# Word conversion at 20 steps an item, six buffers for the first group's columns, GpSimd's DRAIN one row store earlier

## The chip, the cores and the metric

One Trainium2 chip, one NeuronCore. The metric is the device time of one execution in microseconds (us). The engines are named as the profile names them: PE is TensorE (PEld its weight loads), DVE is VectorE, ACT is ScalarE, POOL is GpSimd, SP is SyncE, which here only issues DMAs. SPq and POOLq are the sequencers of SP and POOL.

## The reference, cut to what matters

Pooled attention, then a layer of eight experts of which each token uses one, then a dense layer with the larger of three products. The change lies in the last two.

```python
attn_out = _attn_ref(q, k, v)                       # 8 x 8 heads, 576 tokens, keys pooled by 8
x = attn_out.transpose(0, 2, 1, 3).reshape(4608, 512)
for e in range(8):                                  # experts: 512 -> 1024 -> 512
    mask = expert_idx == e
    h = np.maximum(x[mask] @ w1[e], 0.0)
    out[mask] = gate_w[mask, None] * (h @ w2[e])
h = np.maximum(np.maximum(x @ m1, x @ m2), x @ m3)  # second layer: 512 -> 768, three matrices
return h @ m_out                                    # 768 -> 512
```

## The kernel before

The kernel runs three stages. Attention and routing come first. They are followed by the expert stage: 22 items, of which 18 are pairs (256 tokens) and 4 are singles (128 tokens). Each item has eight pieces, 0 to 3 for the first product (`mm1`, L1090, for singles L1098) and 4 to 7 for the second (`mm2`, L1138, for singles L1122). Every fp32 operand is split into a high and a low part, and three products are taken of the parts. For each piece of a weight, ACT makes `whi` (L1068) and DVE `wlo` (L1070). Behind each `mm1` piece ACT makes `hhi` and DVE `hlo` (L1106). SP loads the raw weights of the next item as soon as a piece has been split.

The second layer's weights are prepared inside the expert stage, in the gaps of DVE and ACT. Two generators do that. `conversions()` (called `cv`) turns the weight words into floats: 48 rows of 256 columns, each row in five steps (L1219, L1232, L1235 with an ACT operation, L1237, L1240). POOL loads the raw words into two buffers, `cvraw`; the load of row n + 2 goes out when L1237 of row n has run (L1238, `load`, L1203). `combinations()` (called `cb`) forms sums and differences of the converted blocks (L1265 to L1278), and POOL stores each 1,792 KB result to `wdram` (L1279). Then it does the same for the output matrix (`wso`, L1302 to L1308), and lastly it runs `columns(0, False)`: the expert stage's result `ybuf` for the first 768 tokens is loaded by SP into `yr` buffers (L1341), six pieces in all, and `sums` (L1358 to L1374) makes the operands `yhl` of the second layer from them.

`between(half, p_)` is called twice in each piece, before and behind its products. When the routing's queue is empty, it advances `cv` by one or two steps and `cb` by one (L1425 to L1427). Whatever is left of both runs behind the last item.

The last stage is `second`: six groups of 768 tokens, nine chunks each. `quad` takes seven products of a chunk into PSUM banks; `snap` (L1688, ACT) copies a partial sum out before a further product is added to its bank; `block` (L1700, L1707, L1708, DVE) forms the maximum of the three matrices. The split of the finished blocks (`ghi` L1727 on ACT, `glo` L1728 and `asum` L1729 on DVE) is kept in the list `parts_` and taken off by `pop(n)` at four points of a quad, by the table `pops` (L1765). `project` multiplies by the output matrix, scales by the gate (`ob`, L1827 on ACT, L1829 on DVE) and stores 128 rows at a time with an indirect DMA of POOL (L1800), six stores in a group. The stores of blocks 0 to 2 follow the products m = 3, those of blocks 3 to 5 the products m = 4. One DRAIN instruction of POOL stands among them (L1833). Each engine takes its instructions in the order of the program.

Of the kernel before, what the change touches and what calls it, by code (L numbers as in the profile page):

```python
# [8 lines left out]
F32 = mybir.dt.float32  # L9
# [12 lines left out]
def attention_moe_moe_kernel(  # L22
# [27 lines left out]
    P = 128  # L50
    B, H, S, D = q.shape
    N, DM = out.shape
    E, _, F = w1.shape
# [66 lines left out]
    if True:  # L120
# [5 lines left out]
        tl = {"w1": [wp1.tile([P, DC, 256], F32, name=f"w1raw{i}") for i in range(4)]}  # L126
# [55 lines left out]
        if True:  # L182
# [761 lines left out]
            def fill(n=1):  # L944

                for _ in range(n):
                    free = [c_ for c_ in queue[0] if c_.state is None] if queue else []
                    if not free:
                        return
                    c_ = free[0]  # L950
                    queue[0].remove(c_)
                    queue[0].append(c_)
                    c_.step()
                    if c_.state == "end":
                        queue[0].remove(c_)
                        if not queue[0]:
                            queue.pop(0)

            def boundary(products=True):

                for c_ in list(queue[0]) if queue else []:
                    if c_.state == "wait":
                        c_.state = None
                    elif c_.state == "pe":
                        c_.state = "products"
                    elif c_.state == "products" and products:
                        c_.step()
# [357 lines left out]
            def columns(g, whole_=True):  # L1325

                w_ = HW if whole_ else HW // 3
                at_ = [(c, n) for c in range(2) for n in range(0, HW, w_)]
                rows = []

                def load(k_):
                    if k_ < len(at_):
                        c, n = at_[k_]
                        t = tl["yr"].tile([P, 2, 2, w_], F32, tag="yr", name=f"yr{g}_{c}_{n}", bufs=2)
                        src = ybuf[:, GW * g : GW * g + GW].rearrange("(i c p) (j n) -> c p i j n", i=2, c=2, j=2)
                        for i in range(2):  # L1340
                            nc.sync.dma_start(t[:, i], src[c, :, i, :, n : n + w_])  # L1341
                        rows.append((t, c, n, w_))

                load(0)
                load(1)
                for _ in range(1 if whole_ else 8):
                    yield
                for k_ in range(len(at_)):
                    yield from sums(*rows[k_])
                    load(k_ + 2)  # L1350

            def sums(t, c, n, w_):
                hi, lo = (x_[:, :, n : n + w_] for x_ in yhl[2 * c : 2 * c + 2])
                tt = nc.vector.tensor_tensor
                b4 = t.rearrange("p i j n -> p (i j) n")
                t_ = tl["yr"].tile([P, 4, w_], F32, tag="ysum", name=uname("ysum"), bufs=1)
                raw = lambda n, m: t_[:, n - 3 : m - 3, :]
                tt(raw(3, 5), b4[:, 1:4:2, :], b4[:, 0:2, :], op=A.subtract)  # L1358
                nc.scalar.copy(hi[:, 0, :], b4[:, 0, :])
                nc.scalar.copy(hi[:, 1:3, :], b4[:, 2:4, :])  # L1360
                yield
                tt(raw(5, 6), b4[:, 3:4, :], raw(3, 4), op=A.subtract)
                tt(raw(6, 7), b4[:, 2:3, :], raw(5, 6), op=A.subtract)
                yield
                nc.scalar.copy(hi[:, 3:7, :], raw(3, 7))
                tt(lo[:, 0, :], b4[:, 0, :], hi[:, 0, :].bitcast(F32), op=A.subtract)
                yield
                tt(lo[:, 1:3, :], b4[:, 2:4, :], hi[:, 1:3, :].bitcast(F32), op=A.subtract)
                yield
                if w_ == HW:  # L1370
                    tt(lo[:, 3:5, :], raw(3, 5), hi[:, 3:5, :].bitcast(F32), op=A.subtract)
                    yield
                n0 = 5 if w_ == HW else 3
                tt(lo[:, n0:7, :], raw(n0, 7), hi[:, n0:7, :].bitcast(F32), op=A.subtract)  # L1374
                yield
# [40 lines left out]
            def between(half, p_=0):  # L1416

                if not routed:
                    return
                if queue:  # L1420
                    if half == 0:
                        boundary(p_ in (0, 1, 2, 3, 7))
                    fill(3)
                else:
                    for _ in range(1 + (p_ % 2 if half else p_ % 4 == 0)):  # L1425
                        next(cv, None)
                    next(cb, None)  # L1427

# [89 lines left out]
            for b in range(1, B):  # L1518
                need = (b // 2) * 9 + (0 if b % 2 == 0 else 4)
                at_ = [need - 7, need - 3, need - 1, need, need, need + 1, need + 2]  # L1520
                at_ = {1: [2, 4, 6, 7], 2: [5, 6, 6, 7, 7, 7, 8, 9, 10]}.get(b, at_[:4] + at_[5:6])
# [102 lines left out]
    CH = F2C // 2 * 3  # L1624
    NCH = CH + 3
    T3 = GB // 2

    def second(st, groups, again=False):
# [10 lines left out]
        def bank(m, name):  # L1639
            x_ = {1: 1, 2: 2, 5: 3}[m]  # L1640
            return pa.tile([P, 512], F32, tag=f"p{x_}", name=name, bufs=2 if x_ == 2 else 3)
# [112 lines left out]
        def quad(g, n, k_):  # L1754
            w_ = wt.pop((g, n))
            nm = f"{g}_{n}"
            p1, p2, p3 = (bank(x_, f"p{x_}_{nm}")[:, 0:HW] for x_ in (1, 2, 5))
            product(p1, w_, 1, True)
            s1 = snap(p1, "s1", f"s1_{nm}")
            product(p3, w_, 5, True)  # L1760
            s5 = snap(p3, "s5", f"s5_{nm}")
            finish_block()
            product(p1, w_, 6, False)
            s2 = snap(p1, "s2", f"s2_{nm}")
            pops = ((3, 1, 1, 3), (1, 0, 0, 0), (0, 0, 1, n < CH - 1))[n % 3]  # L1765
            pop(pops[0])
            product(p2, w_, 2, True)
            block(g, n, (1, 1), (p2, s1))
            pop(pops[1])
            product(p3, w_, 3, False)  # L1770
            block(g, n, (1, 2), (p3, s2))
            pop(pops[2])
            product(p1, w_, 7, False)
            block(g, n, (2, 2), (p1, s5))
            pop(pops[3])

            def last_block():
                product(p1, w_, 4, False)
                load_chunk(k_ + 3)
                block(g, n, (2, 1), (p1,))  # L1780

            late_.append(last_block)
# [29 lines left out]
        def project(g, k0, ahead):  # L1812
            acc, ob = {}, {}
            lo_, hi_ = slice(0, DH), slice(DH, DM)

            def take(m, t):
                if m in (1, 2, 5):
                    acc[m, t] = bank(m, f"o{m}_{g}_{t}")[:, 0:DH]
                if m in (1, 5):
                    j = t if m == 1 else T3 + t  # L1820
                    ob[j] = yp.tile([P, DM], F32, tag="ob", name=f"ob{g}_{j}", bufs=6)
                ps = acc[{1: 1, 6: 1, 7: 1, 4: 1, 5: 5, 3: 5, 2: 2}[m], t]
                out_product(g, m, t, ps)
                j, cols = {1: (t, lo_), 2: (t, lo_), 6: (t, hi_), 3: (t, hi_), 4: (T3 + t, lo_)}.get(m, (T3 + t, hi_))
                dst, gate = ob[j][:, cols], gt[g][:, j : j + 1]
                if m in (1, 5, 6, 4):
                    nc.scalar.activation(dst, ps, AF.Copy, scale=gate)  # L1827
                else:
                    nc.vector.scalar_tensor_tensor(dst, ps, gate, dst, A.mult, A.add)  # L1829
                if m in (3, 4):  # L1830
                    store_rows(g, ob[j], j)
                    if m == 4 and t == 0:
                        nc.gpsimd.drain()  # L1833

            steps = [(1, 0), (1, 1), (5, 0), (1, 2), (5, 1), (5, 2), (6, 0), (6, 1), (6, 2)]
            steps += [(2, 0), (3, 0), (2, 1), (3, 1), (2, 2), (3, 2), (7, 0), (7, 1), (7, 2), (4, 0), (4, 1), (4, 2)]
            for n, (m, t) in enumerate(steps):
                take(m, t)
                if n == 0:
                    pop(3)  # L1840
                elif n == 1:
                    finish_block()
                elif n > 2:
                    pop(3)
                if t == T3 - 1 and m in (6, 3, 4):
                    k_ = (6, 3, 4).index(m)
                    wt.pop((g, CH + k_))
                    load_chunk(k0 + CH + k_ + 3)
                if 5 <= n < 17:
                    next(ahead, None)  # L1850
# [81 lines left out]
```

## Time and profile before

| | |
|---|---|
| median of 3 runs | 1230.9 us (1227.91 to 1232.1) |
| the profiled execution | 1228.26 us, of which the span is 1226.3 us |
| PE busy | 1183.0 us, 96% |
| DVE busy | 884.2 us, 72% |
| ACT busy | 605.4 us, 49% |
| POOL busy | 309.8 us, 25% |

The span is what the profile's clock covers, from the first to the last instruction. The busy time of an engine is the time in which it executes. PE's busy time is drawn from modelled ends of matmuls, so a matmul that is held up shortly can show as a long one.

### The profile page before, as it was taken

The page shows a single profiled execution, that of the slowest core. Times are in us where ns is not written, and L with a number is a line of the kernel's source. Part 1 is how long each engine was busy: PE and PEld are TensorE (multiplying, and loading weights), DVE is VectorE, ACT ScalarE, POOL GpSimd, SP SyncE. Part 2 cuts the span into 40 slices and gives each one's busy share as a digit, 9 for nine tenths or more (in the row PEclk, how much of TensorE's full clock was granted, in tenths as well). Part 3 has the DMA queues.
Part 4 walks back from the last instruction along what each step waited for, and adds up shares of the span by engine and source line. Part 5 has one row for each costly group of instructions (what it writes and reads, how often), then busy time and mean ns, then how long its engine had stood idle before and what let it go on. Part 6 is the DMA issues. An engine that isn't in the chain of part 4 may idle for free.

```text
span 1226.3 us, 23792 instructions
## 1 busy us (share of the span) xinstructions
PE 1183.0 (96%) x8737; PEld 1161.1 (95%) x8737; DVE 884.2 (72%) x1796; ACT 605.4 (49%) x1117; POOL 309.8 (25%) x451
## 2 busy tenths in 40 slices
PE   6899999999999999999999999999999999999997
PEld 5799899999989999999999999999999999999996
DVE  6878977987889999996755368467567557567563
ACT  4666665455666666666655234334334334334332
POOL 7967744201212213213001302104003003003001
PEclk9999999999999999999999999999999999999999
DMA  9998664328865446737539668778769769769763
GB/s 292 241 262 234 176 213 158 121 23 239 277 232 201 148 168 222 265 138 262 177 107 324 233 252 311 290 258 304 283 240 331 260 245 328 272 252 331 267 247 114
DMA packets 108119, 285.10 MB, mean 232 GB/s; under 512 B 17878, under 2 KB 70564, under 8 KB 97628
## 3 DMA queue, kind: packets, MB, share of 16 engines
q1 hardware_dynamic: 87436, 216.40, 51.1%
q0 software_dynamic: 20560, 67.11, 17.8%
q8 instruction: 71, 1.16, 0.4%
q14 instruction: 52, 0.43, 0.1%
HBM read 285.52 MB, written 52.48 MB: 276 GB/s over the span
## 4 chain that ended last, share of the span: by engine, by line
PE 65%; DVE 15%; issue 10%; DMA 5%; ACT 4%; POOL 1%; POOLq 0%; SPq 0%; ACTq 0%; DVEq 0%
PE p L1680 22%; PE py L1138 12%; PE ph L1090 10%; PE o L1792 7%; DVE wlo L1070 3%; PE pav L524 3%; PE ph L1098 2%; PE psc L470 2%; DMA cvraw<-in_moe_w_dram 2%; DVE glo L1728 2%; PE py L1122 2%; PE paT L501 1%; DVE m L1700 1%; PE px L1051 1%; PE pqT L445 1%
## 5 line engine op out<-in xcount | busy, mean ns | idle before, releaser
L1680 PE MATMUL p<-yhi,wt 128*128 128x384 f32 x1512 | 390.4, 337 | 0.6
L1680 PEld LDWEIGHTS p<-yhi,wt 128*128 128x128 f32 x1512 | 273.5, 188 | 4.5 <-ACT s L1688 4.4
L1680 PE MATMUL p<-ylo,wt 128*128 128x384 f32 x756 | 254.1, 336 | 0.0
L1688 ACT COPY s<-p 128x384 f32<-128x384 f32 x162 | 76.5, 480 | 195.9 <-PE p L1680 191.1
L1090 PE MATMUL ph<-xhi,whi 128*128 128x256 f32 x576 | 164.4, 285 | 6.8 <-DVE hlo L1106 5.6
L1090 PE MATMUL ph<-xhi,wlo 128*128 128x256 f32 x576 | 163.2, 283 | 2.1 <-DVE wlo L1070 2.1
L1138 PE MATMUL py<-hhi,wlo 128*128 128x256 f32 x576 | 163.1, 283 | 1.6 <-DVE wlo L1070 1.6
L1138 PE MATMUL py<-hhi,whi 128*128 128x256 f32 x576 | 164.5, 286 | 0.0
L1090 PE MATMUL ph<-xlo,whi 128*128 128x256 f32 x576 | 162.9, 283 | 0.0
L1138 PE MATMUL py<-hlo,whi 128*128 128x256 f32 x576 | 162.9, 283 | 0.0
L1680 PEld LDWEIGHTS p<-ylo,wt 128*128 128x128 f32 x756 | 142.1, 188 | 0.0
L1792 PE MATMUL o<-wt,ghi 128*128 128x256 f32 x756 | 137.6, 283 | 2.2 <-DMA wt<-wdram 0.7
L1707 DVE TENSOR_TENSOR blk<-p,s 128x384 f32<-128x384 f32 x108 | 59.7, 553 | 85.0 <-PE p L1680 85.0
L1792 PEld LDWEIGHTS o<-wt,ghi 128*128 128x128 f32 x756 | 117.2, 189 | 3.9 <-ACT ob L1827 1.6
L1090 PEld LDWEIGHTS ph<-xhi,whi 128*128 128x128 f32 x576 | 110.4, 192 | 8.6 <-DVE hlo L1106 7.3
L1665 POOL DMA_INDIRECT gt<-gbuf,ix x26 | 31.2, 1199 | 325.5 <-DMA ix<-idbuf 187.5
L1090 PEld LDWEIGHTS ph<-xhi,wlo 128*128 128x128 f32 x576 | 110.4, 192 | 2.7 <-DVE wlo L1070 2.7
L1138 PEld LDWEIGHTS py<-hhi,wlo 128*128 128x128 f32 x576 | 110.4, 192 | 2.0 <-DVE wlo L1070 2.0
L1138 PEld LDWEIGHTS py<-hlo,whi 128*128 128x128 f32 x576 | 110.4, 192 | 0.0
L1090 PEld LDWEIGHTS ph<-xlo,whi 128*128 128x128 f32 x576 | 110.4, 192 | 0.0
L1138 PEld LDWEIGHTS py<-hhi,whi 128*128 128x128 f32 x576 | 110.4, 192 | 0.0
L1070 DVE TENSOR_TENSOR wlo<-w2raw,whi 128x1024 fp32r<-128x1024 f32 x84 | 102.2, 1220 | 10.8 <-ACT whi L1068 10.8
(340 smaller groups left out, 2369.2 us busy)
## 6 DMA issues: line engine op xcount, KB each, us to landing
wt<-wdram SPq DMA_DIRECT2D x69, 1792.0 KB
w1raw<-in_moe_w_dram SPq DMA_DIRECT2D x88, 512.0 KB
w2raw<-in_moe_w_dram SPq DMA_DIRECT2D x88, 512.0 KB
wdram<-wst POOLq DMA_DIRECT2D x9, 1792.0 KB
ybuf<-yo SPq DMA_DIRECT2D x40, 256.0 KB
cvraw<-in_moe_w_dram POOLq DMA_DIRECT2D x36, 256.0 KB
xbuf<-x SPq DMA_DIRECT2D x16, 512.0 KB
yr<-ybuf SPq DMA_DIRECT2D x20, 384.0 KB
```

What stands on the lines that cost most here:

```text
L470: nc.tensor.matmul(ps[:, c // 2, (c % 2) * 2 * SP : (c % 2 + 1) * 2 * SP], qT[:, c, :], kbds[segs[0][2] % 3][:, h0 + c].rearrange("p t s - ...
L524: nc.tensor.matmul(ps[lo:hi, bank, (g0 % 4) * DA : (g0 % 4 + g1 - g0) * DA], aT[:, c, lo:hi], vbds[b % 3][:, sl : sl + g1 - g0, :].rearran ...
L1070: eng.tensor_tensor(lo, src, hi.bitcast(F32), op=A.subtract)
L1090: nc.tensor.matmul(ps[:, f, :], a_[:, c, fs], b_[:, c, :], start=(n == 0), stop=(n == 3 * DC - 1))
L1098: nc.tensor.matmul(ps[:, f, 0:P], tl["w1"][piece][:, c, fs], xlo[:, c, 0:P], start=(c == 0), stop=(c == DC - 1))
L1122: nc.tensor.matmul(py[:, 0, :], a_[:, f, 0:P], b_[:, f, :], start=(piece == 0 and f == 0 and n == 0), stop=(last_ and f == 1 and n == 2),)
L1138: nc.tensor.matmul(py[:, c // 2, (c % 2) * 256 : (c % 2 + 1) * 256], a_[:, f, c * P : (c + 1) * P], b_[:, f, :], start=(piece == 0 and f = ...
L1665: nc.gpsimd.indirect_dma_start(out=gt[g][:, j : j + 1], out_offset=None, in_=gbuf[:, :], in_offset=bass.IndirectOffsetOnAxis(ap=cols[j], a ...
L1680: nc.tensor.matmul(ps, a_, b_, start=(start and c + n == 0), stop=(c == 1 and n == 2), skip_group_check=True)
L1688: nc.scalar.copy(t, ps)
L1707: tt(src, add[0], add[1], op=A.add)
L1792: nc.tensor.matmul(ps, a_, b_, start=(m in (1, 2, 5) and c + n == 0), stop=(c == KH - 1 and n == 2), skip_group_check=True,)
```

## The change

Four edits. `between` advances `cv` by one step before each piece's products and by one or two behind them, 20 steps an item; before it was 22, with one more step ahead of pieces 0 and 4. `columns` for the first group allocates six `yr` buffers and issues all six loads at once; before there were two, and each further load went out when a piece had been summed. In `quad` one of the `pop`s of every third chunk moves from behind the third block to ahead of it (this is not in the title). The DRAIN moves from behind the fourth row store (m = 4, t = 0) to behind the third (m = 3, t = 2).

```diff
@@ columns(g, whole_=True)
+                depth = 2 if whole_ else len(at_)
...
-                        t = tl["yr"].tile([P, 2, 2, w_], F32, tag="yr", name=f"yr{g}_{c}_{n}", bufs=2)
+                        t = tl["yr"].tile([P, 2, 2, w_], F32, tag="yr", name=f"yr{g}_{c}_{n}", bufs=depth)
...
-                load(0)
-                load(1)
+                for k_ in range(depth):
+                    load(k_)
                 for _ in range(1 if whole_ else 8):
                     yield
                 for k_ in range(len(at_)):
                     yield from sums(*rows[k_])
-                    load(k_ + 2)
+                    load(k_ + depth)
@@ between(half, p_=0)
-                    for _ in range(1 + (p_ % 2 if half else p_ % 4 == 0)):
+                    for _ in range(1 + (half and p_ % 2)):
                         next(cv, None)
                     next(cb, None)
@@ quad(g, n, k_)
-            pops = ((3, 1, 1, 3), (1, 0, 0, 0), (0, 0, 1, n < CH - 1))[n % 3]
+            pops = ((3, 1, 2, 2), (1, 0, 0, 0), (0, 0, 1, n < CH - 1))[n % 3]
@@ project -> take(m, t)
                 if m in (3, 4):
                     store_rows(g, ob[j], j)
-                    if m == 4 and t == 0:
+                    if m == 3 and t == T3 - 1:
                         nc.gpsimd.drain()
```

On DVE, in the first pair with conversions, this stands between the splits of pieces 2 and 4 before the change (`cvy`, `mraw` are the words in work, `cvraw` the raw ones):

```order
L1070 TENSOR_TENSOR wlo_2_4021<-w1raw_107,whi_2_4020 128x1024
L1237 SCALAR_TENSOR_TENSOR mraw_3849<-cvraw_3861,mraw_3849 128x256
L1240 SCALAR_TENSOR_TENSOR mraw_3849<-cvy_4016,mraw_3849 128x256
L1106 SCALAR_TENSOR_TENSOR hlo_0_4055<-ph_0_4029,hhi_0_4054 128x512
L1219 TENSOR_SCALAR mraw_3849<-cvraw_3953 128x256
L1070 TENSOR_TENSOR wlo_3_4067<-w1raw_108,whi_3_4066 128x1024
L1232 TENSOR_SCALAR cvy_4071<-cvraw_3953 128x256
L1106 SCALAR_TENSOR_TENSOR hlo_1_4099<-ph_1_4073,hhi_1_4098 128x512
L1235 SCALAR_TENSOR_TENSOR cvy_4071<-cvraw_3953,cvy_4071 128x256
L1237 SCALAR_TENSOR_TENSOR mraw_3849<-cvraw_3953,mraw_3849 128x256
L1070 TENSOR_TENSOR wlo_4_4108<-w2raw_2472,whi_4_4107 128x1024
```

With the change, the same place reads:

```order
L1070 TENSOR_TENSOR wlo_2_4019<-w1raw_107,whi_2_4018 128x1024
L1235 SCALAR_TENSOR_TENSOR cvy_4016<-cvraw_3885,cvy_4016 128x256
L1106 SCALAR_TENSOR_TENSOR hlo_0_4051<-ph_0_4025,hhi_0_4050 128x512
L1237 SCALAR_TENSOR_TENSOR mraw_3849<-cvraw_3885,mraw_3849 128x256
L1070 TENSOR_TENSOR wlo_3_4065<-w1raw_108,whi_3_4064 128x1024
L1240 SCALAR_TENSOR_TENSOR mraw_3849<-cvy_4016,mraw_3849 128x256
L1106 SCALAR_TENSOR_TENSOR hlo_1_4096<-ph_1_4070,hhi_1_4095 128x512
L1219 TENSOR_SCALAR mraw_3849<-cvraw_3977 128x256
L1232 TENSOR_SCALAR cvy_4100<-cvraw_3977 128x256
L1070 TENSOR_TENSOR wlo_4_4103<-w2raw_2472,whi_4_4102 128x1024
```

Between `wlo_2` and `wlo_4` six conversion operations have become five, one row per two pieces, so that a row now begins at the same place in every second piece.

On DVE, in the quad of chunk 3 of the first group, these are the second and third block (`m`) with the parts among them, before:

```order
L1700 TENSOR_TENSOR m_0_3_9675<-p_0_3_9620,s_0_3_9652 128x384
L1728 TENSOR_TENSOR glo_9410<-asum_9596,ghi_9409 128x384
L1700 TENSOR_TENSOR m_0_3_9685<-p_0_3_9618,s_0_3_9635 128x384
L1728 TENSOR_TENSOR glo_9410<-m_0_0_9485,ghi_9409 128x384
L1729 TENSOR_TENSOR asum_9596<-m_0_0_9514,asum_9596 128x384
```

And with the change (its lines are one higher):

```order
L1701 TENSOR_TENSOR m_0_3_9675<-p_0_3_9620,s_0_3_9652 128x384
L1729 TENSOR_TENSOR glo_9410<-asum_9596,ghi_9409 128x384
L1729 TENSOR_TENSOR glo_9410<-m_0_0_9485,ghi_9409 128x384
L1701 TENSOR_TENSOR m_0_3_9687<-p_0_3_9618,s_0_3_9635 128x384
L1730 TENSOR_TENSOR asum_9596<-m_0_0_9514,asum_9596 128x384
```

The third block stands one operation later; the last `asum` keeps its place.

On SP, the six `yr` pieces now stand together, behind the stores of item 16 and ahead of a weight load for item 18 (`w1raw_107`); before, the first two stood one item earlier, ahead of the second of item 17's weight loads (`w1raw_106`), and the others apart:

```order
L1180 DMA ybuf<-yo_1_8467 128x2x256
L1342 DMA yr_0_0_8483<-ybuf 128x2x128 x2
L1342 DMA yr_0_128_8486<-ybuf 128x2x128 x2
L1342 DMA yr_0_256_8489<-ybuf 128x2x128 x2
L1342 DMA yr_1_0_8492<-ybuf 128x2x128 x2
L1342 DMA yr_1_128_8495<-ybuf 128x2x128 x2
L1342 DMA yr_1_256_8498<-ybuf 128x2x128 x2
L1017 ISA
L1017 REGISTER_ALU
L1017 ISA
L1017 DMA w1raw_107<-in_moe_w_dram 128x4x256
```

Twelve DMA issues moved past the stores of item 16 on SP's queue, and the conversions' end moved with them by about one item.

## Rows read from the trace of the kernel before

**Rows 1.** Busy time by stage: length, then PE, PEld, DVE, ACT, POOL, clock, DMA.

```profile
268.00:545.00 277.00, 269.48 (x2235) 267.25 (x2234) 250.87 (x463) 174.40 (x256) 59.58 (x77) 1.00 0.63 207
545.00:624.00 79.00, 79.00 (x664) 79.00 (x663) 59.57 (x85) 47.18 (x73) 13.51 (x16) 1.00 0.56 187
624.00:679.00 55.00, 54.32 (x385) 49.60 (x383) 26.26 (x34) 29.25 (x48) 8.48 (x9) 1.00 0.78 265
```

**Rows 2.** Two of six places where PE stands still, and the sum of all six.

```profile
284.00:290.00 6.00, 4.63 (x39) 4.42 (x38) 3.39 (x7) 3.00 (x6) 2.61 (x3) 1.00 0.82 256
354.00:366.00 12.00, 9.27 (x73) 8.66 (x73) 10.16 (x21) 8.18 (x14) 3.20 (x4) 1.00 0.48 151
...
sum 42.00, PE 34.64 PEld 32.81 DVE 36.17 ACT 26.67 POOL 15.12; mean PE 5.77 PEld 5.47 DVE 6.03 ACT 4.45 POOL 2.52
```

**Rows 3.** DVE's groups by form, 268 to 545 us: busy, mean ns, idle before.

```profile
L1240 DVE SCALAR_TENSOR_TENSOR mraw<-cvy,mraw 128x256 f32<-128x256 f32 x48 | 20.2, 421 | 0.7
L1219 DVE TENSOR_SCALAR mraw<-cvraw 128x256 int32<-128x256 int32 x48 | 14.2, 296 | 8.8 <-DMA cvraw<-in_moe_w_dram 7.8 <-DMA cvraw<-in_moe_w_out_dram 1.0
```

**Rows 4.** POOL in order of time: start, length, idle before and its releaser.

```profile
343.38 0.57 POOL L1279 DMA_DIRECT2D wdram<-wst  x1 [2.10 <-DVE wst L1278]
347.53 0.57 POOL L1203 DMA_DIRECT2D cvraw<-in_moe_w_dram  x1 [3.58 <-DVE mraw L1237]
```

**Rows 5.** DVE in order of time: the two longest of six waits for raw words.

```profile
287.64 0.29 DVE L1219 TENSOR_SCALAR mraw<-cvraw 128x256 int32<-128x256 int32 x1 [2.61 <-DMA cvraw<-in_moe_w_dram]
355.74 0.29 DVE L1219 TENSOR_SCALAR mraw<-cvraw 128x256 int32<-128x256 int32 x1 [3.04 <-DMA cvraw<-in_moe_w_dram]
```

**Rows 6.** The chain that ended last: the last pair and the first single begin.

```profile
600.89 11.52 PE ph L1090 x96
...
624.37 7.15 PE ph L1098 x64
```

**Rows 7.** DVE's column sums of the first group, 560 to 679 us (line L1374).

```profile
L1374 DVE TENSOR_TENSOR ylo<-ysum,yhi x6: 681/684/693, 592.6 to 627.3; 128x512 fp32r<-128x512 f32 x6
```

**Rows 8.** SP's queue in order of time: a column load and weight loads behind it.

```profile
602.86 1.03 SPq L1341 DMA_DIRECT2D yr<-ybuf  x2
604.74 3.48 SPq L1017 DMA_DIRECT2D w1raw<-in_moe_w_dram  x2
```

**Rows 9.** The quads of chunks 3 and 4: DVE and ACT in order of time.

```profile
707.98 0.55 DVE L1700 TENSOR_TENSOR m<-p,s 128x384 f32<-128x384 f32 x1
708.45 0.55 DVE L1728 TENSOR_TENSOR glo<-m,ghi 128x384 fp32r<-128x384 f32 x1
709.50 0.52 ACT L1727 CAST ghi<-asum 128x384 fp32r<-128x384 f32 x1 [1.93 <-DVE asum L1729]
709.92 0.85 ACT L1688 COPY s<-p 128x384 f32<-128x384 f32 x2
```

**Rows 10.** PEld's waits from 679 us on: total, times, longest.

```profile
PEld p L1680 <- ACT s L1688: 4.4, 12, 0.4
```

**Rows 11.** The last four row stores on POOL, in order of time.

```profile
1211.62 0.98 POOL L1800 DMA_INDIRECT out_dram<-ob,ix  x1 [1.17 <-DVE ob L1829]
1215.86 0.98 POOL L1800 DMA_INDIRECT out_dram<-ob,ix  x1 [3.25 <-ACT ob L1827]
1220.18 0.98 POOL L1800 DMA_INDIRECT out_dram<-ob,ix  x1 [3.33 <-issue]
1221.47 0.99 POOL L1800 DMA_INDIRECT out_dram<-ob,ix  x1 [0.30 <-issue]
```

**Rows 12.** The DRAIN (L1833): all six, then the last alone; ns min/median/max, starts.

```profile
L1833 POOLq DRAIN  x6: 3662/7075/13893, 767.2 to 1215.6; - x6
L1833 POOLq DRAIN  x1: 3662/3662/3662, 1215.6 to 1215.6; - x1
```

**Rows 13.** ACT's last three results; the first and the last of them.

```profile
1215.11 0.47 ACT L1827 ACTIVATE ob<-o,gt 128x256 f32<-128x256 f32 x1 [10.32 <-PE o L1792]
...
1217.27 0.47 ACT L1827 ACTIVATE ob<-o,gt 128x256 f32<-128x256 f32 x1 [0.61 <-PE o L1792]
```

## The prediction

> **What bounds the kernel now.** I read the busy shares first: PE works 96% of the span, so only two things can shorten the kernel: gaps in PE's work, and what lies behind PE's last product. The table by stage says where the gaps are. From 268 to 545 us, while the words are converted, PE is busy 269.5 of 277 us: 7.5 us are lost, with DVE busy 250.9 us, 91% [rows 1]. From 545 to 624 us nothing is lost, and 0.7 us in the singles up to 679 us [rows 1]. Six short places hold 42.00 - 34.64 = 7.4 us of the 7.5; the two worst are 284 to 290 us (1.4 us) and 354 to 366 us (2.7 us) [rows 2]. In the first of them DVE itself is busy only 3.4 of 6 us, so it was not overworked but waiting [rows 2]. For what, DVE's rows tell: it waited 2.61 us and 3.04 us for raw words (`cvraw`) just there [rows 5], and 8.8 us in the window for them in all [rows 3]. POOL's rows give the history of the second: the load went out at 347.53 us, behind a 1,792 KB store issued at 343.38 us [rows 4], and DVE had it at 355.74 us [rows 5], 8.2 us later. DVE takes its work in order, so the splits queued behind that row come late, and PE stops.
>
> The tail is the other place. The last products' results leave ACT from 1215.11 us on, the last at 1217.27 + 0.47 = 1217.74 us [rows 13], but the fifth and sixth row stores begin at 1220.18 and 1221.47 us [rows 11]. Between them and the fourth stands the DRAIN, from 1215.6 us for 3.66 us, to 1219.3 us [rows 12]. The span ends at 1226.3 us, 3.84 us behind the sixth store (1221.47 + 0.99).
>
> **The conversions' pace.** 48 rows of five steps are 240 steps: 240 / 22 = 10.9 items before, 240 / 20 = 12 now. A pair takes 624.37 - 600.89 = 23.5 us of pure PE work [rows 6]; with the losses, 270 us for 10.9 items is 24.7 us. Two effects follow. First, between the issue of a `cvraw` load and its use lie six steps (two rows ahead, issued in a row's fourth step). A step lasted 24.7 / 22 = 1.12 us, so 6.7 us; now about 24.2 / 20 = 1.21 us, 7.3 us. Every load gets 0.6 us more, against the 8.2 us that one took. Secondly, DVE has 0.4 rows less in an item. A row is two operations of 0.30 us and three of 0.42 us [rows 3], 1.9 us busy (records overlap a little, so 1.5 to 1.9): 0.6 to 0.75 us less per item.
>
> Price: the two worst places lose 0.6 us of wait each, 1.2 us; the second has a backlog on DVE behind the wait (10.2 of 12 us busy), from which the lighter load takes another 0.6 us. The other four places hold 7.4 - 1.4 - 2.7 = 3.3 us, with DVE nearly full (the sum less the two rows: 36.17 - 3.39 - 10.16 = 22.6 of 24 us) [rows 2]; I take half, 1.6 us. That is 3.4 us off 7.5, and 1.1 more items at the loss that stays (4.1 / 10.9 = 0.4 us) give 0.4 us back. Net gain 3.0 us. Bounds: 7.5 us if every gap closes; below, a loss, which is the first rival.
>
> At this place a page speaks against me. The Trainium skill, DMA: Bandwidth & Descriptors, section Anatomy of one DMA (SWDGE path), gives a load from GpSimd about 2.0 us and its bytes at 436 GB/s; for 256 KB an estimate from that page is 2.6 us. By that rule no load would be late at either pace, and only DVE's lighter load would count. The trace disagrees: 8.2 us, with other transfers in flight.
>
> **What slides behind.** The conversions end about 20 us later (12 x 24.2 = 290 against 270 us), and the output matrix's split and the column sums with them. The split then falls where the stage lost nothing beside the same work (545 to 624 us) [rows 1]: no cost. The column sums ended at 627.3 + 0.7 = 628 us [rows 7]; 20 us later, with the shorter singles, is 645 us or so. PE needs them at 679 us, so 34 us of cover stay. They now lie mostly in the singles, where DVE is busy 26 of 55 us and ACT 29 [rows 1]; some 20 steps of about 0.4 us (a fifth of a sum's operations, the largest 0.68 us [rows 7]) add 8 us. For splits that come late in one or two singles I take 0.2 us, 0 to 1.
>
> **Six buffers.** The six loads are twelve DMAs in a row on SP, 0.5 us each (1.03 us for two [rows 8]): 6 us. Queued behind them are the first single's weight loads, which went out at 604.74 us [rows 8] and now go at about 609 us; PE wants these third and fourth pieces not before 628 us (four pieces in 7.15 us from 624.37 us [rows 6]). 15 us of cover or more for a 4 us delay: nothing. The sums no longer wait for a freed buffer, but nobody waited for the sums: no gain either.
>
> **The moved pop.** In every third chunk the third block stands one `glo` later on DVE, 708.45 - 707.98 = 0.47 us. Behind it PE waits for that block before it adds another product to its bank; the block would end at about 709.0 us where the next product of that bank starts at about 709.2 us. PE does lose there, 0.35 us in each of twelve quads [rows 10], but to ACT: the copy `s` starts at 709.92 us, because ACT sits before it in a `ghi` that waited 1.93 us for the last `asum` [rows 9], and the next product on that bank waits for the copy. That `asum` keeps its rank on a DVE that runs without a gap, so the copy starts when it did. I take 0. Bounds: 4.4 us gained if that wait went, 12 x 0.47 = 5.6 us lost if the whole shift reached PE.
>
> **The DRAIN.** In the first five groups POOL's stores have the next group's time to land; no one waits. In the last group it now follows the store of 1211.62 us. Before, it ended 1219.3 - (1215.86 + 0.98) = 2.45 us behind the end of the store ahead of it; by that it now ends at 1211.62 + 0.98 + 2.45 = 1215.05 us. The fourth result is ready at 1215.11 + 0.47 = 1215.58 us [rows 13], so the fourth store starts at 1215.86 us as before. The next follow at the distance of the last two, 1.29 us [rows 11]: 1217.15 and 1218.44 us (the last result, at 1217.74 us, is there). The sixth moves from 1221.47 to 1218.44 us: 3.0 us, and the end with it. Bounds: 0 (the end hangs on something else) to 3.3 us.
>
> **Sum.** 3.0 + 3.0 - 0.2 = 5.8 us less than the profiled execution's 1228.26 us: 1222.5 us. That execution lies 2.6 us below the median of 1230.9 us, to which the same step gives 1225.1 us. I predict 1225 us.
>
> **Rivals.** (1) Slower: the new pace is five steps in two pieces, so every row now meets the same splits and the same products, four times an item, where before it drifted. If that place is a bad one, each of 12 items loses; now it is 7.5 / 10.9 = 0.7 us an item. With the tail's 3.0 us in hand the change is even at (7.5 + 3.0) / 12 = 0.9 us. At 1.4 us, the loss of 284 to 290 us in every item, it is 16.8 - 7.5 - 3.0 = 6 us slower, 1237 us. Against it: most items of before lost far less, and the DVE work between two splits is more even. (2) The pace buys nothing: loads are late because of the traffic, and 0.6 us doesn't matter. Then 12 items lose 8.2 us, and 3.0 - 0.7 - 0.2 = 2.1 us are left: 1229 us. (3) The DRAIN waits for more than one store and lasts as in other groups, 7.1 us in the median [rows 12]: it ends at about 1218.5 us, the stores follow as before, and the tail gains nothing: 1228 us. Against it: in that last group only 3.66 us were needed. (4) Loads are never late, only DVE's load counts, worth about 1 us: 1230.9 - 1.0 - 3.0 + 0.4 + 0.2 = 1227.5 us. That is the page's rule. (5) The lighter DVE closes all gaps: 7.5 + 3.0 = 10.5 us, 1220.4 us.
>
> **Chances.** Forecast 0.50; rivals 0.08, 0.17, 0.08, 0.05, 0.12. A measurement of this kernel can tell about 0.3%, 3.7 us, from no change. Faster by more (under 1227.2 us): nearly all of the forecast (its own range is 1222.5 to 1227.5), all of (5), half of (3) and (4), a little of (2): 0.69. Slower (over 1234.6 us): rival (1), 0.08. The same: 0.23. The range goes from 1220 to 1230 us: it holds the forecast, most of (2), (3) and (4), half of (5), and leaves (1) out.
>
> **What would show it.** The wait of L1219 for `cvraw` falls from 8.8 us to about 5; PE's loss in the conversions falls from 7.5 to about 4.5 us over a window some 20 us longer; the last DRAIN starts at about 1211.5 us less what the expert stage gave, and the last three stores stand 1.29 us apart. `PEld` still waits twelve times for ACT's `s`. I am wrong if the waits for raw words grow, if PE stands still in the singles, or if the end lies 6 us behind the last store.

## The result, and the profile after

The changed kernel takes 1222.25 us in the median of 6 runs (1217.98 to 1226.13), the kernel before 1231.56 us beside it: a ratio of 0.992, 95% interval 0.9891 to 0.9948, and the medians lie 9.3 us apart. The forecast was 1225 us, in a range of 1220 to 1230 us.

The profiled execution took 1222.45 us with a span of 1220.5 us, 5.8 us less than before. Busy time by stage of the changed kernel, with the columns of [rows 1], over the two places of [rows 2], the conversions, and the stretch from there to the end of the singles:

```profile
284.00:290.00 6.00, 6.00 (x53) 6.00 (x52) 4.46 (x10) 3.32 (x5) 2.71 (x3) 1.00 0.77 133
354.00:366.00 12.00, 12.00 (x103) 12.00 (x102) 10.67 (x20) 8.84 (x14) 3.50 (x4) 1.00 0.55 177
...
268.00:565.00 297.00, 297.00 (x2488) 297.00 (x2487) 265.55 (x485) 190.63 (x276) 61.16 (x80) 1.00 0.60 197
565.00:668.00 103.00, 101.78 (x783) 96.62 (x782) 66.07 (x99) 60.56 (x100) 14.29 (x19) 1.00 0.76 253
```

The last row of the conversions now ends at 555.8 us (538.9 us before), and PE has no gap in them: the 7.5 us of [rows 1] are gone. From 565 to 668 us it loses 1.2 us. Before, it lost nothing there.

DVE's waits, from 268 to 545 us, by engine, line and what came last, with total, times and longest, first of the kernel before and then of the changed one:

```profile
DVE wlo L1070 <- ACT whi L1068: 9.9, 12, 2.0
DVE mraw L1219 <- DMA cvraw<-in_moe_w_dram: 7.8, 5, 3.0
DVE hlo L1106 <- ACT hhi L1105: 1.3, 3, 0.6
DVE mraw L1219 <- DMA cvraw<-in_moe_w_out_dram: 1.0, 1, 1.0
```

```profile
DVE wlo L1070 <- ACT whi L1068: 15.4, 15, 2.0
DVE hlo L1106 <- ACT hhi L1105: 5.2, 14, 0.6
DVE mraw L1219 <- DMA cvraw<-in_moe_w_dram: 3.9, 4, 1.2
DVE mraw L1219 <- DMA cvraw<-in_moe_w_out_dram: 1.6, 1, 1.6
```

The raw words are waited for less (5.5 us against 8.8). The larger difference is in the splits: 14 times, where it was 3, DVE stands at `hlo` before ACT has its half. DVE is early where it was late.

The chain that ended last, at the places of [rows 6], and SP's queue, at that of [rows 8]:

```profile
593.01 11.54 PE ph L1090 x94
...
616.51 3.59 PE ph L1098 x32
...
672.73 8.29 PE p L1681 x42
```

```profile
598.42 8.19 SPq L1342 DMA_DIRECT2D yr<-ybuf  x12
607.03 0.60 SPq L1017 DMA_DIRECT2D w1raw<-in_moe_w_dram  x2
```

The last pair begins 7.9 us earlier, and the first single 7.9. The twelve column loads take SP 8.2 us. The weights behind them go out 2.3 us later than in [rows 8] by the clock of the span, but the last pair begins 7.9 us earlier, so against the work they are 10.2 us late (14.0 us behind the pair's first product, 3.8 before). PE waits for neither.

The tail: ACT's last result, POOL's last row stores and the last DRAIN, for [rows 11 to 13]:

```profile
1213.36 0.47 ACT L1828 ACTIVATE ob<-o,gt 128x256 f32<-128x256 f32 x1 [0.60 <-PE o L1793]
```

```profile
1207.72 0.98 POOL L1801 DMA_INDIRECT out_dram<-ob,ix  x1 [1.18 <-DVE ob L1830]
1211.96 0.98 POOL L1801 DMA_INDIRECT out_dram<-ob,ix  x1 [3.26 <-ACT ob L1828]
1213.24 0.98 POOL L1801 DMA_INDIRECT out_dram<-ob,ix  x1 [0.30 <-issue]
1214.53 0.98 POOL L1801 DMA_INDIRECT out_dram<-ob,ix  x1 [0.30 <-issue]
```

```profile
L1834 POOLq DRAIN  x1: 3261/3261/3261, 1207.5 to 1207.5; - x1
```

The last DRAIN starts at 1207.5 us and lasts 3.26 us, to 1210.8, before ACT has its first of the last three results; three stores follow ACT's results 1.29 us apart. The sixth ends 1.68 us behind ACT's last result (1213.83 us) and not 4.72 us. But the span ends at 1220.5 us, 4.99 us behind the sixth store, where it was 3.84 us.

That the span fell by 5.8 us, the sum of the prediction, is a coincidence, as this table of one profiled execution of every kernel shows. It gives the times from the experts' first product (`mm1`, first L1090) to the first of the last stage (L1680, L1681), from there to the end of ACT's last result, and from there to the end of the span. The ratio is against runs of the kernel before on the same chip (its medians went from 1227.2 to 1231.6 us from chip to chip, so the ratios are to be compared, not the medians).

| kernel | median us | ratio, 95% | experts | last stage | tail |
|---|---|---|---|---|---|
| before | 1230.9 | | 504.9 | 538.8 | 8.6 |
| before, again | 1227.7 (one run) | | 504.4 | 537.8 | 8.7 |
| pace alone | 1227.1 | 1.0003 (0.9994 to 1.0013) | 505.3 | 537.4 | 8.7 |
| pace, uneven | 1227.2 | 1.0002 (0.9992 to 1.0013) | 506.0 | 537.7 | 8.8 |
| six buffers alone | 1229.0 | 1.0009 (1.0001 to 1.0018) | 505.1 | 537.6 | 8.7 |
| pace and six buffers | 1220.0 | 0.9947 (0.9931 to 0.9963) | 497.2 | 537.5 | 8.8 |
| pop alone | 1227.6 | 1.0001 (0.9993 to 1.001) | 506.3 | 537.7 | 8.7 |
| DRAIN alone | 1225.0 | 0.9978 (0.997 to 0.9987) | 504.6 | 537.3 | 6.7 |
| three raw buffers | 1220.9 | 0.9953 (0.9936 to 0.997) | 499.3 | 537.5 | 8.8 |
| three raw buffers, DRAIN | 1219.7 | 0.9938 (0.9923 to 0.9953) | 498.9 | 537.4 | 7.5 |
| the change | 1222.25 | 0.992 (0.9891 to 0.9948) | 497.4 | 541.2 | 6.7 |
| the change, again | 1218.6 (one run) | | 497.7 | 538.2 | 6.5 |
| the change, three raw buffers | 1217.7 | 0.9922 (0.9907 to 0.9938) | 497.7 | 537.7 | 7.4 |
| the change, no DRAIN | 1223.1 | 0.9968 (0.9958 to 0.9979) | 497.2 | 538.0 | 11.4 |

The change takes 7 us off the expert stage and 2 off the tail, 9 us together. Its first profiled execution lost 3 us in the last stage, which its second does not show, nor either of the two kernels built on it. The six runs of the change go from 1217.98 to 1226.13 us; how many of them carry that loss is not known.

### The profile page after: what moved, and what is told of

Its sections match the earlier page's. It is cut to its first block, busy times and chain, and to the rows that moved or that the text cites. A ratio compares the mean times of both kernels' runs of the same rounds, so it can differ in the third digit from the quotient of the medians.

```text
span 1220.5 us, 23787 instructions
## 1 busy us (share of the span) xinstructions
PE 1183.4 (97%) x8737; PEld 1161.2 (95%) x8737; DVE 879.6 (72%) x1796; ACT 605.8 (50%) x1117; POOL 306.4 (25%) x451
## 4 chain that ended last, share of the span: by engine, by line
PE 77%; issue 9%; DVE 6%; DMA 4%; ACT 2%; POOL 1%; SPq 1%; POOLq 0%; DVEq 0%; ACTq 0%
PE p L1681 27%; PE py L1138 15%; PE ph L1090 15%; PE o L1793 6%; PE pav L524 3%; PE ph L1098 2%; PE psc L470 2%; PE py L1122 1%; PE px L1051 1%; PE paT L501 1%; DMA wdram<-wso 1%; DMA qgrp<-in_q_dram 1%; DMA wt<-wdram 1%; DVE wlo L1070 1%; PE pqT L445 1%
## 5 line engine op out<-in xcount | busy, mean ns | idle before, releaser
L1681 PE MATMUL p<-yhi,wt 128*128 128x384 f32 x1512 | 391.0, 337 | 0.8 <-DVE m L1701 0.5
L1681 PEld LDWEIGHTS p<-yhi,wt 128*128 128x128 f32 x1512 | 273.8, 188 | 5.3 <-ACT s L1689 4.2
L1681 PE MATMUL p<-ylo,wt 128*128 128x384 f32 x756 | 254.1, 336 | 0.0
L1090 PE MATMUL ph<-xhi,whi 128*128 128x256 f32 x576 | 163.6, 284 | 0.7 <-DVE hlo L1106 0.7
L1090 PE MATMUL ph<-xhi,wlo 128*128 128x256 f32 x576 | 163.2, 283 | 0.8 <-DVE wlo L1070 0.7
L1090 PE MATMUL ph<-xlo,whi 128*128 128x256 f32 x576 | 162.9, 283 | 0.0
L1681 PEld LDWEIGHTS p<-ylo,wt 128*128 128x128 f32 x756 | 142.1, 188 | 0.0
L1090 PEld LDWEIGHTS ph<-xhi,wlo 128*128 128x128 f32 x576 | 110.5, 192 | 1.2 <-DVE wlo L1070 1.2
L1090 PEld LDWEIGHTS ph<-xhi,whi 128*128 128x128 f32 x576 | 110.5, 192 | 0.9 <-DVE hlo L1106 0.9
L1070 DVE TENSOR_TENSOR wlo<-w2raw,whi 128x1024 fp32r<-128x1024 f32 x84 | 102.1, 1219 | 12.0 <-ACT whi L1068 10.2
L1090 PEld LDWEIGHTS ph<-xlo,whi 128*128 128x128 f32 x576 | 110.5, 192 | 0.0
```

The source lines that it names most:

```text
L1070: eng.tensor_tensor(lo, src, hi.bitcast(F32), op=A.subtract)
L1090: nc.tensor.matmul(ps[:, f, :], a_[:, c, fs], b_[:, c, :], start=(n == 0), stop=(n == 3 * DC - 1))
L1681: nc.tensor.matmul(ps, a_, b_, start=(start and c + n == 0), stop=(c == 1 and n == 2), skip_group_check=True)
```

## The experiments

The theory after the result was that the pace closes the gaps and the DRAIN shortens the tail, and that the six buffers and the pop do nothing. First each part was made alone.

**Pace alone.**

```diff
-                    for _ in range(1 + (p_ % 2 if half else p_ % 4 == 0)):
+                    for _ in range(1 + (half and p_ % 2)):
```

> Only the pace: cv gets 20 steps an item, all else as before. Theory pace (raw words come in time and DVE has less to do): PE's loss between 268 us and the conversions' end falls from 7.5 us to under 2 us, DVE's wait for raw words from 8.8 us to about 5, about 1 to 2 us come back as a loss in the singles; 5 us faster. Rival (the profile after had a lucky run, the pace is worth nothing): loss 6 to 8 us, same time.

Measured: 1227.1 us, ratio 1.0003, no gain at all. Yet PE's gaps in the conversions are gone. The stages, from 268 to 565 and from there to 668 us:

```profile
268.00:565.00 297.00, 297.00 (x2486) 296.86 (x2486) 265.02 (x483) 190.97 (x276) 61.73 (x80) 1.00 0.63 199
565.00:668.00 103.00, 97.07 (x726) 91.92 (x725) 61.58 (x92) 54.97 (x92) 13.35 (x15) 0.97 0.73 236
```

What was won is given back behind the conversions: 5.9 us. PE's waits from 600 to 690 us, DVE and SP in order of time, and the busy time in slices of 2 us (PE, PEld, DVE, ACT, POOL, granted clock, DMA) show where:

```profile
PE ph L1098 <- DVE hlo L1106: 4.4, 1, 4.4
```

```profile
631.59 0.69 DVE L1374 TENSOR_TENSOR ylo<-ysum,yhi 128x512 fp32r<-128x512 f32 x1
637.96 0.42 DVE L1358 TENSOR_TENSOR ysum<-yr 128x256 f32<-128x256 f32 x1 [5.67 <-DMA yr<-ybuf]
638.58 0.42 DVE L1106 SCALAR_TENSOR_TENSOR hlo<-ph,hhi 128x256 fp32r<-128x256 f32 x1 [0.20 <-ACT hhi L1105]
```

```profile
627.50 1.80 SPq L1017 DMA_DIRECT2D w2raw<-in_moe_w_dram  x2
629.35 0.94 SPq L1341 DMA_DIRECT2D yr<-ybuf  x2
```

```profile
634.00:636.00 2.00, 0.70 (x7) 0.51 (x5) 0.00 (x0) 0.00 (x0) 0.00 (x0) 1.00 0.93 367
636.00:638.00 2.00, 0.00 (x0) 0.00 (x0) 0.04 (x1) 0.44 (x2) 0.00 (x0) 0.83 1.03 336
638.00:640.00 2.00, 0.94 (x4) 0.95 (x5) 1.50 (x5) 1.46 (x4) 0.00 (x0) 0.50 0.08 25
640.00:642.00 2.00, 2.00 (x12) 2.00 (x11) 1.33 (x3) 1.40 (x3) 0.00 (x0) 0.50 0.61 154
642.00:644.00 2.00, 2.00 (x11) 2.00 (x11) 1.68 (x3) 1.13 (x2) 0.00 (x0) 0.50 0.84 250
644.00:646.00 2.00, 2.00 (x15) 1.88 (x15) 1.45 (x2) 0.84 (x3) 0.00 (x0) 0.96 0.90 268
```

With two `yr` buffers, the last column load goes out at 629.35 us, when its buffer is free and behind the next single's weights. DVE waits for it until 637.96 us. The split `hlo` that the single needs is queued behind that wait, so PE stands still for 4.4 us. Then the granted clock is 0.50, the lower of its two levels (1.2 GHz), until about 644 us: some 2.5 us of PE's time more (half of the 0.94, 2.00 and 2.00 us that PE worked at it, and a little from 644 us on). In the conversions DVE waited 9.2 us for raw words, not less than before, while PE lost nothing:

```profile
DVE mraw L1219 <- DMA cvraw<-in_moe_w_dram: 6.5, 7, 2.2
DVE hlo L1106 <- ACT hhi L1105: 4.8, 13, 0.6
DVE mraw L1219 <- DMA cvraw<-in_moe_w_out_dram: 2.7, 1, 2.7
```

So it isn't the shorter wait that closes the gaps. Here too DVE is early at 13 `hlo`.

**DRAIN alone.**

```diff
-                    if m == 4 and t == 0:
+                    if m == 3 and t == T3 - 1:
                         nc.gpsimd.drain()
```

> Only the DRAIN's place, all else as before. Theory drain: the last three stores stand 1.29 us apart, the sixth begins about 1.2 us behind the start of ACT's last result in place of 4.2 us, and the kernel is 2 to 3 us faster. Rival (the end is set by what lands, so three stores in a row only make the end come later behind the last of them): the sixth store is 3 us earlier and the end less than 1 us.

Measured: 1225.0 us, ratio 0.9978, 2.7 us faster (1.6 to 3.7). The tail of its trace is 1.8 us shorter than in [rows 11 to 13]: ACT's last result at 1216.56 us, the end at 1223.3.

**The pop alone.**

```diff
-            pops = ((3, 1, 1, 3), (1, 0, 0, 0), (0, 0, 1, n < CH - 1))[n % 3]
+            pops = ((3, 1, 2, 2), (1, 0, 0, 0), (0, 0, 1, n < CH - 1))[n % 3]
```

> Only the moved pop, all else as before. Theory: nothing, PEld still waits twelve times for ACT's s, 4 to 4.5 us in all, and the time is within 1.5 us. Rival (the third block's 0.47 us reaches PE): waits of PE for DVE's m in twelve quads, 3 to 5 us slower.

Measured: 1227.6 us, ratio 1.0001: nothing.

**Six buffers alone** (the edits of `columns` in the diff above, nothing else).

> Only the six column buffers, all else as before. Theory: nothing, since nobody waits for the sums: PE loses nothing between 545 and 679 us but the 0.7 us at its end, the time is within 1.5 us. Rival (twelve DMAs in a row hold up the weight loads behind them on SP): PE waits for a split between 575 and 625 us, 1 to 3 us slower.

Measured: 1229.0 us, ratio 1.0009: nothing, or a microsecond lost. In the order of before, the sums have time in the last pair, and buffers are not missed.

**Three raw buffers.** The kernel before, 22 steps an item, with the loads one row further ahead.

```diff
-  raws[n] = tl["cv"].tile([P, W, 2], I32, tag="cvraw", name=f"cvraw{n}", bufs=2)
+  raws[n] = tl["cv"].tile([P, W, 2], I32, tag="cvraw", name=f"cvraw{n}", bufs=3)
...
+                load(2)
...
-                    load(n + 2)
+                    load(n + 3)
```

> The kernel before with three buffers for raw words, each load one row earlier, pace 22. Theory late loads (PE's losses come from DVE waiting for raw words): DVE's wait for raw words falls from 8.8 us to under 2, PE's loss in the conversions from 7.5 to under 3 us, 4 us faster. Theory DVE load (DVE simply has too much to do at 22 steps): the waits fall as well, but PE's loss stays at 5 to 8 us and the time is the same.

Measured: 1220.9 us, ratio 0.9953, 5.8 us faster. The first step of a row (L1219; lines are one higher here) waits for no load any more. The conversions of its trace, and PE's waits from 268 to 680 us:

```profile
268.00:565.00 297.00, 294.75 (x2453) 293.19 (x2452) 271.74 (x482) 190.15 (x277) 69.31 (x89) 1.00 0.66 214
```

```profile
PE ph L1090 <- DVE hlo L1106: 2.1, 5, 0.5
```

At 22 steps late raw words cost 5.3 of the 7.5 us of [rows 1]; 2.2 us stay, five short waits for `hlo`, with no late load ahead of them.

**Pace, uneven.** The kernel before with 20 steps an item, but the single and double steps elsewhere: the extra ones ahead of pieces 0 and 4 stay, and those behind pieces 3 and 7 go.

```diff
-                    for _ in range(1 + (p_ % 2 if half else p_ % 4 == 0)):
+                    for _ in range(1 + (p_ in (1, 5) if half else p_ % 4 == 0)):
```

> The kernel before with 20 steps an item, but spread unevenly: the extra steps of before ahead of pieces 0 and 4 stay, and of those behind the odd pieces only 1 and 5 keep theirs, so three of the four extra steps of a half item fall on its first two pieces. Theory pace: as with the even 20, PE's loss in the conversions under 2 us, 5 us faster. Rival order (it is the even spread, one row in two pieces, that helps): PE's loss stays at 4 us or more and at least half of the gain is gone.

Measured: 1227.2 us, ratio 1.0002, as pace alone: no gap in the conversions, and one of 5.1 us in the singles, 4.6 us of it from 635 to 640 us. Between these two orders, where in an item the steps stand made no difference to the time; their number did.

**Before and the change, again.** Both kernels unchanged, one execution each.

> The kernel before, once more, for the scatter of its profile: if the loss of PE in the conversions is a property of the program, it is 6 to 9 us again, at about the same places; if it is luck of one execution, it can be anything from 1 us up.

> The changed kernel, once more, for the scatter of its profile: PE's loss in the conversions under 1.5 us again, 1 to 2.5 us in the singles, and the end 4 to 5 us behind the last store. If the 541 us of the last stage were luck, they are nearer to the 538.8 us of before.

Measured: 1227.7 and 1218.6 us. Before loses 6.8 us in the conversions, of them 2.7 us again at 354 to 366 us and 0.6 us at 284 to 290 us; the change loses none, and no 3 us in its last stage. The gaps belong to the program; that loss did not come again.

**Pace and six buffers.** Both edits as above, in the kernel before.

> The kernel before with two edits: 20 steps an item, and six buffers for the first group's columns. Theory (the new pace closes the gaps in the conversions, and the six buffers keep the columns that now fall into the singles from holding DVE and with it PE near 635 us): 7 us faster than before, ratio about 0.994; from the first product of the experts to the first of the last stage some 497.5 us in place of 504.8, no gap near 635 us, no dip of the granted clock behind it. Rival A (the two edits are each worth nothing, so together nothing, and all that the change gained is the DRAIN's): ratio about 1.000. Rival B (the stall near 635 us is not from late column pieces): the gap of 4 us stays, ratio about 0.999.

Measured: 1220.0 us, ratio 0.9947, 6.5 us faster (4.5 to 8.5). Two edits that alone give nothing give this together. The stages of its trace:

```profile
268.00:565.00 297.00, 297.00 (x2488) 297.00 (x2487) 265.25 (x483) 191.03 (x275) 60.97 (x80) 1.00 0.62 199
565.00:668.00 103.00, 101.78 (x778) 96.38 (x778) 66.86 (x99) 59.81 (x99) 15.72 (x19) 1.00 0.79 254
```

The 4.4 us gap and the dip of the clock are gone (1.00 where pace alone had 0.97). The expert stage is 8.1 us shorter than with pace alone: 4.7 us of PE's idle time (5.9 - 1.2), about 2.5 us at the lower clock, and a remainder.

**Three raw buffers, DRAIN.** Both edits as above, in the kernel before, 22 steps.

> The kernel before, 22 steps an item, with a third buffer for raw words (each load goes out three rows ahead of its use) and the DRAIN behind the third store. Theory (the late raw words cost 5 to 6 us of the expert stage, the DRAIN 2.0 us of the tail, and the two are independent): 8 us faster than before, ratio about 0.9935, no wait of L1219 for raw words in the pairs, end 6.7 us behind ACT's last result in place of 8.6. Rival (part of the third buffer's gain is the tail's in another guise): about 6 us, ratio 0.995.

Measured: 1219.7 us, ratio 0.9938, 7.6 us faster (5.8 to 9.5): nearer to the theory, but the interval holds both. The tail is 7.5 us where 6.7 was expected, 1 us shorter than in the kernel before.

**The change, three raw buffers.** The changed kernel with the edit of three raw buffers.

> The changed kernel with the third buffer for raw words added. Theory (at 20 steps PE already loses nothing in the conversions, so a load that comes earlier frees nothing that PE waits for): the same as the changed kernel within 1 us, though the waits of L1219 for raw words vanish (5.5 us in the changed kernel). Rival (the raw words that still come late set something that PE waits for, in the conversions or behind them): 2 us or more faster than the changed kernel.

Measured: 1217.7 us, ratio 0.9922, where the change has 0.992: the same within what these runs tell (the change ran beside other runs of before). No wait for raw words is left, and PE's idle time is what it was. At 20 steps the late loads, up to 2.8 us in these traces, cost nothing.

**The change, no DRAIN.** The changed kernel without `nc.gpsimd.drain()`.

```diff
                     store_rows(g, ob[j], j)
-                    if m == 3 and t == T3 - 1:
-                        nc.gpsimd.drain()
```

> The changed kernel with no DRAIN among the row stores at all. Theory (moved behind the third store, the last DRAIN has ended before ACT has the fourth result, so that it holds no store any more, and the five others always had time): the same as the changed kernel within 1 us; the last three stores stand 1.29 us apart as in the changed kernel, the end about 6.7 us behind ACT's last result. Rival (the end waits for what the DRAIN waited for, so that its removal moves a wait to the end, or gives the 1.2 us back by which the end hangs longer behind the last store): the end comes 8 us or more, or about 5.5 us, behind ACT's last result.

Measured: 1223.1 us, ratio 0.9968, some 6 us slower than the change by the two ratios, 5.4 us slower than the kernel of the section above, which ran on the same chip, and 4.8 us by the tails. The rival holds. POOL's last stores, of a span that ends at 1221.2 us:

```profile
1207.88 0.98 POOL L1801 DMA_INDIRECT out_dram<-ob,ix  x1 [3.26 <-ACT ob L1828]
1209.17 0.98 POOL L1801 DMA_INDIRECT out_dram<-ob,ix  x1 [0.30 <-issue]
1210.46 0.98 POOL L1801 DMA_INDIRECT out_dram<-ob,ix  x1 [0.30 <-issue]
```

The stores stand as in the change, but the end comes 9.8 us behind the last one, 4.8 us later than in the change, where the last DRAIN took 3.26 us. So leaving the DRAINs out saves nothing: the end comes later by more than the last of them took. Which of the six matter, no run shows.

## Why the prediction was right, and where its steps were not

The direction came as forecast, and 1222.25 us lies in the stated range, but just under the 1222.5 to 1227.5 us that I gave the forecast itself, and nearer to rival (5) with 1220.4 us. The sum saved 5.8 us and the medians say 9.3: three terms were mis-sized, and one step failed.

**Pace, forecast 3.0 us; 7 us with the six buffers.** That the gaps were DVE's waits for raw words and what queued up behind them was right in the main: three raw buffers alone win 5.3 of the 7.5 us. The price was wrong in how the pace helps. I let every load gain 0.6 us, kept half of the rest, and expected waits of about 5 us and a loss of 4.5 us. The waits follow the pace only in part (8.8 to 12.2 us in the five traces with 22 steps and two raw buffers, 5.5 to 10.1 us in the six with 20), and yet PE loses 5.9 to 8.2 us in each of the five and nothing in any of the six. This is rival (5), which I gave 0.12. Pace alone is the wait of before (9.2 against 8.8 us) with the lighter load on DVE, and it has no gap: the load does it. The lead that DVE has over PE shows it directly. The product of a piece takes the PSUM bank of the piece two before it, so PE can begin it only when `hlo` of that earlier piece has been made. In the same pair, first before and then with pace alone:

```profile
386.46 0.68 DVE L1106 SCALAR_TENSOR_TENSOR hlo<-ph,hhi 128x512 fp32r<-128x512 f32 x1
387.20 0.39 PE L1090 MATMUL ph<-xhi,whi 128*128 128x256 f32 x1 [0.55 <-DVE hlo L1106]
```

```profile
378.95 0.68 DVE L1106 SCALAR_TENSOR_TENSOR hlo<-ph,hhi 128x512 fp32r<-128x512 f32 x1
380.98 0.28 PE L1090 MATMUL ph<-xhi,whi 128*128 128x256 f32 x1
```

Before, PE stands 0.55 us and begins as `hlo` ends; with pace alone `hlo` has been done for 1.35 us. Over all pairs from 268 to 552 us (pieces 0 and 1) the median of this lead is 0.15 to 0.40 us in the five traces with 22 steps and two raw buffers, 0.64 and 0.65 us in the two at 22 with three, 1.02 us at the uneven 20, and 1.35 us in the five other two-buffer traces at 20. So 0.4 rows less in an item give DVE twice the lead that it has at 22 steps even when no load is late. That this lead is what a late load is paid from follows from these rows; no run varies it by itself.

**Six buffers, forecast nothing: the step that failed.** Alone they are worth nothing, as forecast. But I wrote that nobody waited for the sums and counted 34 us of cover until the last stage reads them. The sums slide into the singles by the pace itself, and DVE takes its work in order: a sum that waits for its load holds the split of the single behind it, which PE wants at once (5.67 us of DVE's wait became 4.4 us of PE's). I had asked who needs the sums, and not who stands behind them. "I am wrong if PE stands still in the singles" is what happens when only that edit is missing.

**What slid behind, forecast 0.2 us (0 to 1) in all; 1.2 us.** Before lost nothing from 565 to 668 us. In the singles the changed kernel loses 0.7 us, at 625 to 630 us, where DVE, with the sums among its splits, is busy 4.97 of 5 us. Another 0.5 us goes at 585 to 595 us, still in the pairs, and that is the output matrix's split, to which I gave no cost: ACT waits there to make `wso` until an earlier store of it has landed, and the `whi` behind it, DVE's `wlo` and PE come late.

```profile
586.72 0.83 ACT L1302 CAST wso<-osum 128x768 fp32r<-128x768 f32 x1 [2.36 <-DMA wdram<-wso]
```

**The DRAIN, forecast 3.0 us; about 2** (the five tails with it are 6.5 to 7.5 us, the eight with it behind the fourth store 8.6 to 8.8; alone it won 2.7 us, 1.6 to 3.7). The stores moved as worked out, 3.04 us nearer to ACT's last result, 1.29 us apart. But the end lies 4.8 to 5.8 us behind the last store in the five traces with the DRAIN behind the third, and 3.84 to 3.91 us in the eight with it behind the fourth. One store more stands behind the DRAIN, and a microsecond or more goes to the end. That the end keeps its distance from the last store was the part of that step that didn't hold. Rival (3) falls: the last DRAIN was short.

**The pop, forecast nothing: nothing.** PEld still waits twelve times for ACT's `s`, as in [rows 10]:

```profile
PEld p L1681 <- ACT s L1689: 4.2, 12, 0.4
```

**The other rivals.** Rival (1), a row locked to a bad place, falls: two 20-step orders with rows at different places have no gap at all. Rival (2), a pace that buys nothing, came true for pace alone, but for another reason. Rival (4), the rule of the Trainium skill (DMA: Bandwidth & Descriptors, section Anatomy of one DMA, SWDGE path), by which no load would be late, does not agree with these runs. A load of the changed kernel was issued right behind a 1,792 KB store, at 514.75 us, and DVE had it at 521.87 us: 7.1 us, against an estimate of 2.6 us from that page.

```profile
514.20 0.56 POOL L1279 DMA_DIRECT2D wdram<-wst  x1 [6.50 <-DVE mraw L1237]
514.75 0.54 POOL L1203 DMA_DIRECT2D cvraw<-in_moe_w_out_dram  x1
```

```profile
521.87 0.29 DVE L1219 TENSOR_SCALAR mraw<-cvraw 128x256 int32<-128x256 int32 x1 [1.56 <-DMA cvraw<-in_moe_w_out_dram]
```

**The sum.** Expert stage 6.7 to 7.7 us (504.4 and 504.9 against 497.2 to 497.7) and tail 2 us make 8.7 to 9.7 us. The times say the same: pace with six buffers 6.5 us and the DRAIN alone 2.7 us are 9.2 us, the medians 9.3. That 1225 us came so near is in part luck: the expert stage's gain was forecast 4 us too small (3.0 - 0.2 us, against about 7) and the DRAIN's 1 us too large, so the two errors partly cancel.

## What to carry to other kernels

When background work is slowed down it ends later, so ask what stands behind its last steps on an engine that works in order, not only who reads their result: here that was worth the whole gain of 7 us. A gain by one edit can be hidden by a stall that another edit of the same change removes, so parts that measure as nothing alone belong in a run together before they are dropped. A wait on the engine that feeds PE cost nothing here as long as that engine was early otherwise; look at how long before its use a result is ready, not only at how long the engine waits for a late load.

## What the runs showed of the hardware that was not expected

- A gap of 4.4 us on PE was followed by 6 us at half of the full clock (0.50 from 638 to 644 us in pace alone), so it cost some 2.5 us beyond itself, an estimate from the slices above. The gaps of [rows 2], 1.4 and 2.7 us in all, left the clock at 1.00. But the longest of them, 1.84 to 1.85 us in all five traces with 22 steps and two raw buffers, was followed by a granted clock of 0.50 in two of the five (six buffers alone from 366 to 368 us, DRAIN alone from 364 to 366 us): the same short gap sometimes costs clock and sometimes does not.
- The end came later behind POOL's last row store the more row stores had no DRAIN behind them: 3.8 to 3.9 us with two of them (eight traces), 4.8 to 5.8 us with three (five traces), 9.8 us with none of the 36 drained (one trace). That the end waits for these stores is how I read it. The six DRAINs together take some 5 us off the end (a tail of 6.7 us in the change, 11.4 without them).
